# Decay-delta attention with a gated expert: chunks of 32 tokens, one batch per strip of partitions

## The chip, the cores and the metric

The kernel runs on one core of a Trainium2 chip. The metric is the device time of one launch in microseconds (us), median of several runs. TensorE (PE) multiplies, VectorE (DVE), ScalarE (ACT) and GpSimd (POOL) work on elements, and all transfers are issued from the queue of SyncE (SP).

## The reference

Two stages follow each other. The first is a recurrence over 768 tokens for each of 4 batches and 8 heads, with a state of 40 x 40 per head:

```python
y[:, :, t] = np.einsum('bhd,bhde->bhe', rt, state)
Sa = np.einsum('bhde,bhe->bhd', state, at)
state_decay = state * wt[:, :, None, :] - np.einsum('bhd,bhe->bhde', Sa, bt)
state = state_decay + np.einsum('bhd,bhe->bhde', vt, kt)
```

The second takes `y` as x of shape (4, 768, 320) and computes `h = relu(x @ w_in)` (1024 columns), a convolution of 3 taps along the tokens, `gate = sigmoid(conv)`, and `(h * gate) @ w_out` (320 columns). All in float32; the weights come as doubles.

## The kernel before

The recurrence is worked in chunks of C = 64 tokens. Inside a chunk the rule of the state is a unit triangular system for each head, so a chunk needs the scores of its tokens on each other, the inverse of a triangular matrix, a chain of products that carries the state on, and the outputs. A step takes one chunk of two batches; the four batches are two halves (`NP = 2`), worked one after the other, and there are 24 steps `m`, two to a window of 128 tokens.

- `scores` (L305 to L366): transposes of `k`, `b`, `a` on PE (`pk`, `pa`, `pz`), products `ps` of all 64 + 64 rows of `k` and `b` against `a` (L358), and `at`, masked on DVE (L363).
- `solve_in` and `solve` (L369 to L418): the diagonal blocks of 32 x 32 go from `at` to DRAM (`bd`, L373) and come back spread over partitions (`bb`, L381). 31 steps of elimination on POOL follow, each a product `st` (L402) and a sum `xx` (L408). The inverses go out (`xd`, L410) and come in as `tt` (L416).
- `chain` (L423 to L480): for one batch pair's half, the old state against `ah` (L436), the scores against `v` (L445), copy to `psb`, the inverse against that (L453), copy to `vu`. This is done for the first 32 tokens and again for the other 32, so each chunk has two such rounds. The state is then moved on with `pu` (L465, L473, L475).
- `outputs` (L484 to L566): `pr`, `pv`, `pt` are transposes, `pm` (L527) the scores of `r`, `py` (L541, L546) the outputs, `xf`, `xh`, `xl` the columns for the expert.
- `moe_in`, `moe_out` (L587 to L668): `ph` (L606) multiplies the window by both parts of `w_in`, `po` (L651) by both parts of `w_out`.

A product in float32 is two passes on PE, each with its own load of weights: 768 products at L453 are 1536 passes in the profile. Those of the expert, in a narrower float32 form, and the transposes take one pass.

Each part of a step is a generator that yields a few times. The dictionary `T` gives, for each kind of part, the step at which it is meant to stand; the parts are sorted by that and advanced in turn, which gives a first order. The framework's list scheduler then sets the order within each engine's queue (`schedule_with_timeline_sim=True`). Every engine works its queue in order, and so does SP's: a transfer that waits holds back those behind it. Buffers are rings (`bufs`), and a load waits until the readers of the buffer's last contents are done.

Of the kernel before, what the change touches and what calls it, by code (L numbers as in the profile page):

```python
# [17 lines left out]
C = 64  # L18
HB = 32
NZ = 4  # L20
NL = dict(w=1, a=1, r=2, kb=5, vu=3)
NWA = 5
NSUF, NPRE, NAT, NBB, NTT = 4, 6, 3, 2, 3
NAH, NKT, NAP, NVT, NRP, NSN, NMS, NRC = 7, 2, 2, 1, 1, 2, 2, 1
X = dict(k0=1, s0=0, xl=1, tg=0, rp=0, xx=1, cc=0)
NPS = dict(P=1, U=1, A=2, B=2, M=2)
T = dict(
    lwa=-3.686, lr=-0.08, dec=-3.09, lkb=-2.577, lv=-0.106, sc=-2.165, scb=0.413, scl=-0.145,
    so=-1.19, sol=0.564, chb=0.051, chl=0.412, ou=0.872, oub=0.433, oul=0.597, moe=4.134,
    moef=0.446, moel=0.444, mo0=0.197, moo=0.544, mwa=-1.3, mw0=-0.026, mw1=2.5, mop=0.324,  # L30
    decb=0.2,
)
GC = (0, 120, 200)
# [4 lines left out]
def tile_decay_delta_attention_then_conv_gate_moe(  # L38
# [19 lines left out]
    NB = 2  # L58
    NP = B // NB
    NW = S // (2 * C)  # L60
    NPAIR = NF // 2
    G = 3
    GR = 3 * D

# [3 lines left out]
    so = ctx.enter_context(tc.tile_pool(name="so", bufs=1))  # L68
    ch = ctx.enter_context(tc.tile_pool(name="ch", bufs=2))
    s1 = ctx.enter_context(tc.tile_pool(name="s1", bufs=2))  # L70
    mo = ctx.enter_context(tc.tile_pool(name="mo", bufs=2))
    gp = ctx.enter_context(tc.tile_pool(name="gp", bufs=4))
    dr = ctx.enter_context(tc.tile_pool(name="dr", bufs=2, space=DRAM))
    psP = ctx.enter_context(tc.tile_pool(name="psP", bufs=NPS["P"], space=PSUM))
    psU = ctx.enter_context(tc.tile_pool(name="psU", bufs=NPS["U"], space=PSUM))
    psA = ctx.enter_context(tc.tile_pool(name="psA", bufs=NPS["A"], space=PSUM))
    psB = ctx.enter_context(tc.tile_pool(name="psB", bufs=NPS["B"], space=PSUM))
    psM = ctx.enter_context(tc.tile_pool(name="psM", bufs=NPS["M"], space=PSUM))

# [15 lines left out]
    for q in range(2):  # L95
        nc.gpsimd.affine_select(
            out=tri[q * C : q * C + C, :], in_=tri[q * C : q * C + C, :],
            compare_op=ALU.is_ge, fill=0.0,
            base=-1, pattern=[[1, C]], channel_multiplier=-1,
        )  # L100
    xini = cp.tile([128, HB // NZ, HB], BF16, name="xini")
    nc.gpsimd.memset(xini, 1.0)
    for z in range(NZ):
        zs = slice(z * 128 // NZ, (z + 1) * 128 // NZ)
        nc.gpsimd.affine_select(
            out=xini[zs], in_=xini[zs], compare_op=ALU.is_equal, fill=0.0,
            base=-z, pattern=[[-NZ, HB // NZ], [1, HB]], channel_multiplier=0,
        )
    SL = C + 1
    NS = 2 * G  # L110
    dsuf = cp.tile([GR, NS * SL], BF16, name="dsuf")
    nc.vector.memset(dsuf, 0.0)
    nc.vector.memset(dsuf.rearrange("p (s c) -> p s c", c=SL)[:, :, C : C + 1], 1.0)
    dp0 = cp.tile([GR, NS * SL], F32, name="dp0")
    nc.vector.memset(dp0, 0.0)
    wxs = []
    for i in range(2):
        t = cp.tile([GR, NS * SL + 1], F32, name=f"wx{i}")
        nc.vector.memset(t, 0.0)
        wxs.append(t)  # L120

# [7 lines left out]
    def from_f64(raw, e, t, m):  # L129
        """Words of doubles (low, high) to float32, rounded to nearest; below its range to zero."""  # L130
# [29 lines left out]
    def load_moe_weights():  # L160
# [35 lines left out]
        # heads 5, 3, 4, 6, 7 of the low part move to where a row of x meets them (see moe_pack)  # L196
# [21 lines left out]
    def cols(bi, g):  # L218
        return slice(bi * H * D + GC[g], bi * H * D + GC[g] + GR)

    def src(x, p, lo, ln):
        xs = x[p * NB : (p + 1) * NB, :, lo : lo + ln, :]
        return xs.rearrange("b h t d -> t (b h) d")

    def flat(t):
        return t.rearrange("p h d -> p (h d)")

# [1 line left out]
    def hold(t):  # L229
        """The load of t comes after the first scores, which its bytes would delay."""  # L230
        nc.vector.tensor_copy(t[0:1, 0, 0:1], sts[0]["at"][0:1, 1, 0, 0:1])

    def load_wa(wd):
        p, n, t0 = wd["p"], wd["n"], wd["wi"] * 2 * C
        for x, nm in ((w, "w"), (a, "a")):
            t = ld.tile([128, NB * H, D], F32, tag=nm, bufs=NL[nm], name=f"{nm}n{n}")
            if n == 1 and nm == "w":
                hold(t)
            nc.sync.dma_start(t, src(x, p, t0, 2 * C))
            wd[nm] = flat(t)  # L240
        yield

    def load_r(wd):
        p, n, t0 = wd["p"], wd["n"], wd["wi"] * 2 * C
        t = ld.tile([128, NB * H, D], F32, tag="r", bufs=NL["r"], name=f"rn{n}")
        if n == 0:
            hold(t)
        nc.sync.dma_start(t, src(r, p, t0, 2 * C))
        wd["r"] = flat(t)
        yield  # L250

    def load_kb(st):
        wd, m = st["wd"], st["m"]
        t0 = wd["wi"] * 2 * C + st["c"] * C
        t = ld.tile([128, NB * H, D], F32, tag="kb", bufs=NL["kb"], name=f"kb{m}")
        if 1 < m < NL["kb"]:
            hold(t)
        nc.sync.dma_start(t[0:C], src(k, wd["p"], t0, C))
        nc.sync.dma_start(t[C:128], src(b, wd["p"], t0, C))
        st["kb"] = flat(t)  # L260
        yield

    def load_v(st):
        wd, m = st["wd"], st["m"]
        t0 = wd["wi"] * 2 * C + st["c"] * C
        t = ld.tile([128, NB * H, D], F32, tag="vu", bufs=NL["vu"], name=f"vu{m}")
        if 0 < m < NL["vu"]:
            hold(t)
        nc.sync.dma_start(t[0:C], src(v, wd["p"], t0, C))
        st["vu"] = flat(t)  # L270
        yield

# [1 line left out]
    def decays(wd, bi):  # L274
        n = wd["n"]
        pool, tag = (psM, "M") if n == 0 and bi == 1 else (psA, "A")
        pw = pool.tile([128, G, 128], F32, tag=tag, name=f"pw{n}{bi}")
        for g in range(G):
            nc.tensor.transpose(pw[:GR, g, :], wd["w"][:, cols(bi, g)], ident)
        wx = wxs[bi]  # L280
        nc.scalar.copy(
            wx[:, : NS * SL].rearrange("p (s c) -> p s c", c=SL)[:, :, 1:SL],
            pw[:GR].rearrange("p g (c t) -> p (g c) t", c=2),
        )
        yield
        suf = wn.tile([GR, NS * SL], F32, tag="suf", bufs=NSUF, name=f"suf{n}{bi}")
        nc.vector.tensor_tensor_scan(
            out=suf[:, ::-1], data0=wx[:, 1 : NS * SL + 1][:, ::-1],
            data1=dsuf[:, ::-1], initial=0.0, op0=ALU.mult, op1=ALU.add,
        )  # L290
        wd["suf"][bi] = suf.rearrange("p (g c t) -> p g c t", c=2, t=SL)
        nc.vector.reciprocal(
            dp0.rearrange("p (s c) -> p s c", c=SL)[:, :, 0:1],
            suf.rearrange("p (s c) -> p s c", c=SL)[:, :, 0:1],
        )
        pre = wn.tile([GR, NS * SL], F32, tag="pre", bufs=NPRE, name=f"pre{n}{bi}")
        nc.vector.tensor_tensor_scan(
            out=pre, data0=wx[:, : NS * SL], data1=dp0,
            initial=0.0, op0=ALU.mult, op1=ALU.add,
        )  # L300
        wd["pre"][bi] = pre.rearrange("p (g c t) -> p g c t", c=2, t=SL)
        yield

# [1 line left out]
    def scores(st, bi):  # L305
        wd, c, m, kb = st["wd"], st["c"], st["m"], st["kb"]
        sf = wd["suf"][bi]
        pool, tag = (psM, "M") if m == 0 and bi == 1 else (psA, "A")
        if bi == 0:
            st["at"] = wn.tile([128, NB, H, C], F32, tag="at", bufs=NAT, name=f"at{m}")  # L310
        wc = wn.tile([GR, G, 3], F32, tag=f"wc{bi}", bufs=NAT + 1, name=f"wc{m}{bi}")
        nc.vector.tensor_tensor(
            wc, sf[:, :, c, 0:1].to_broadcast([GR, G, 3]),
            hmask.unsqueeze(1).to_broadcast([GR, G, 3]), ALU.mult,
        )
        st["wc"][bi] = wc
        pk = pool.tile([128, G, 128], F32, tag=tag, name=f"pk{m}{bi}")
        for g in range(G):
            nc.tensor.transpose(pk[:GR, g, :], kb[:, cols(bi, g)], ident)
        if m == 0 and X["k0"]:  # L320
            kt = gp.tile([128, 512], F32R, tag="gl", name=f"kt{m}{bi}").bitcast(F32)
            kt = kt[:GR, : G * 128].rearrange("p (g t) -> p g t", g=G)
        else:
            kt = s1.tile([GR, G, 128], F32, tag="kt", bufs=NKT, name=f"kt{m}{bi}")
# [98 lines left out]
    def chain(st, nxt, bi):  # L423
# [35 lines left out]
        if last:  # L459
            yield  # L460
            return
# [378 lines left out]
```

## Time and profile before

Times of three runs: 833.13 us median, 832.01 to 842.79.

| the profiled execution | |
|---|---|
| span, first to last instruction | 831.5 us (1.6 below the median of the runs) |
| mean granted TensorE clock | 0.901 |
| PE busy, passes | 750.8 us (90%), 7645 |
| weight loads (PEld) busy | 667.7 us (80%) |
| DVE, ACT, POOL busy | 491.2, 404.5, 497.7 us |
| DMA packets, bytes | 237,619, 59.05 MB |

The page gives for each engine the time in which it was busy; a group's mean duration of an instruction on PE is its latency, and passes overlap, so that what a pass costs is read from groups that follow each other without a gap. SPq rows are the issuing of transfers on SP's queue.

### The profile page before, as it was taken

To read this page: it belongs to the slowest core of one execution; us is meant where nothing else is said; L and a number is where in the kernel's file an instruction comes from. 1 tells how busy PE (TensorE), PEld (TensorE's weight loads), DVE (VectorE), ACT (ScalarE), POOL (GpSimd) and SP (SyncE) were. 2 spreads that over 40 slices of the span, in tenths; PEclk is the share of its full clock that TensorE was granted. 3 is DMA by queue.
4 is the path that set the end of the run, shared out by engine and by line. 5 is a ranking of instruction groups with operands and counts; after the bars stand their busy time and mean duration, and the time that the engine had idled before them with its cause. 6 is when DMAs were issued, how large, how long until landed. Compare 5 with 4: busy or idle time off the path is not lost.

```text
span 831.5 us, 19927 instructions
## 1 busy us (share of the span) xinstructions
PE 750.8 (90%) x7645; PEld 667.7 (80%) x7645; DVE 491.2 (59%) x1236; ACT 404.5 (49%) x956; POOL 497.7 (60%) x1513
## 2 busy tenths in 40 slices
PE   5453969779988999999999999999799999999987
PEld 4343858669877889899898998898798998988986
DVE  6693858546545756666566476556366564663634
ACT  3121224336435646555556575465265465554644
POOL 1378885505888458787678478677655875781000
PEclk9555557897996999999999999999899999999989
DMA  8875453330441352532533543423334323211000
GB/s 140 136 150 93 102 91 59 59 74 17 88 85 30 67 103 59 99 68 48 106 68 60 101 81 74 89 56 77 64 65 86 73 43 74 53 21 30 10 17 25
DMA packets 237619, 59.05 MB, mean 71 GB/s; under 512 B 225788, under 2 KB 231828, under 8 KB 237524
## 3 DMA queue, kind: packets, MB, share of 16 engines
q1 hardware_dynamic: 237524, 57.78, 36.7%
q8 instruction: 60, 0.98, 0.5%
q14 instruction: 35, 0.29, 0.1%
HBM read 44.92 MB, written 10.22 MB: 66 GB/s over the span
## 4 chain that ended last, share of the span: by engine, by line
PE 69%; POOL 12%; DMA 11%; issue 3%; DVE 2%; ACT 1%; SPq 1%; ACTq 0%; POOLq 0%
PE ph L606 10%; PE po L651 9%; PE pp L453 7%; PE pp L445 7%; POOL xx L408 6%; POOL st L402 6%; PE ps L358 5%; PE py L546 5%; DMA xd<-xx 4%; PE pm L527 4%; PE py L541 3%; PE pu L465 3%; PE pp L436 3%; DMA tt<-xd 3%; PE pv L513 2%
## 5 line engine op out<-in xcount | busy, mean ns | idle before, releaser
L402 POOL TENSOR_TENSOR st<-xx,bb 128x60 f32<-128x60 f32 (+24 forms) x744 | 245.7, 331 | 159.7 <-DMA bb<-bd 95.5
L408 POOL TENSOR_TENSOR xx<-xx,st 128x60 f32<-128x60 f32 (+24 forms) x744 | 248.9, 336 | 54.5
L453 PE MATMUL pp<-psb,tt 32*32 32x40 f32 x1536 | 77.7, 205 | 29.3 <-DMA tt<-xd 28.8
L453 PEld LDWEIGHTS pp<-psb,tt 32*32 32x32 f32 x1536 | 65.7, 113 | 42.3 <-DMA tt<-xd 30.1
L457 ACT COPY vu<-pp 32x320 f32<-32x320 f32 x96 | 40.0, 417 | 95.1 <-PE pp L453 94.5
L450 ACT COPY psb<-pp 32x320 f32<-32x320 f32 x96 | 39.8, 415 | 88.8 <-PE pp L445 88.4
L502 DVE TENSOR_TENSOR rp<-pr,hmask 120x192 f32<-120x192 f32 x144 | 42.6, 350 | 65.0 <-PE pr L494 64.0
L445 PE MATMUL pp<-vu,at 96*32 96x40 f32 (+1 forms) x1536 | 78.3, 208 | 0.5 <-ACT vu L457 0.5
L445 PEld LDWEIGHTS pp<-vu,at 96*32 96x32 f32 (+1 forms) x1536 | 66.3, 116 | 12.5 <-issue 2.2
L358 PE MATMUL ps<-ap,kt 120*128 120x192 f32 (+1 forms) x288 | 66.6, 376 | 2.9 <-DVE kt L325 2.3
L344 ACT ACTIVATE ap<-ah,hmask 120x192 f32<-120x192 f32 x144 | 55.2, 445 | 23.2 <-DVE ah L337 20.3
L358 PEld LDWEIGHTS ps<-ap,kt 120*128 120x128 f32 x288 | 56.2, 227 | 6.8 <-DVE kt L325 2.7
L606 PE MATMUL ph<-xh,wih 120*128 120x256 f32 x288 | 56.6, 303 | 5.7 <-ACT xh L562 5.7
L546 PE MATMUL py<-kb,ms 128*64 128x40 f32 x768 | 57.4, 236 | 0.1
L546 PEld LDWEIGHTS py<-kb,ms 128*64 128x64 f32 x768 | 52.6, 145 | 3.5 <-issue 1.6
L527 PE MATMUL pm<-rp,vt 120*128 120x192 f32 (+1 forms) x288 | 53.3, 324 | 0.5 <-ACT sn L522 0.5
L629 DVE SCALAR_TENSOR_TENSOR cc<-hb,cw,cc 128x256 f32<-128x256 f32 x96 | 45.0, 496 | 11.4 <-ACT cc L625 11.4
L527 PEld LDWEIGHTS pm<-rp,vt 120*128 120x128 f32 x288 | 48.4, 199 | 1.1 <-ACT sn L522 0.8
L606 PEld LDWEIGHTS ph<-xh,wih 120*128 120x128 f32 x288 | 43.7, 198 | 6.8 <-ACT xh L562 6.0
L639 DVE TENSOR_TENSOR cc<-cc,hb 128x512 f32<-128x512 f32 x48 | 34.0, 713 | 21.8 <-ACT cc L638 21.4
L533 DVE TENSOR_TENSOR ms<-pm,tri 128x512 f32<-128x512 f32 x48 | 33.0, 688 | 22.4 <-PE pm L527 21.9
L633 DVE SCALAR_TENSOR_TENSOR cc<-hb,cw,cc 128x256 f32<-128x256 f32 x96 | 45.9, 495 | 0.0
(710 smaller groups left out, 1656.1 us busy)
## 6 DMA issues: line engine op xcount, KB each, us to landing
bb<-bd SPq DMA_DIRECT2D x24, 512.0 KB
wn<-in_w_dram SPq DMA_DIRECT2D x12, 320.0 KB
an<-in_a_dram SPq DMA_DIRECT2D x12, 320.0 KB
kb<-in_k_dram SPq DMA_DIRECT2D x24, 160.0 KB
kb<-in_b_dram SPq DMA_DIRECT2D x24, 160.0 KB
vu<-in_v_dram SPq DMA_DIRECT2D x24, 160.0 KB
rn<-in_r_dram SPq DMA_DIRECT2D x12, 320.0 KB
out_dram<-ob SPq DMA_DIRECT2D x20, 160.0 KB
```

Source lines behind the costliest of these rows:

```text
L344: nc.scalar.activation(out=ap[:, :, h, :], in_=ah, func=AF.Copy, scale=hmask[:, h : h + 1])
L358: nc.tensor.matmul(ps[:, h0 : h0 + hi - lo, :], kt[:, g, :], ap[:, g, lo:hi, :], start=(g == 0), stop=(g == G - 1), skip_group_check=True,)
L402: eng.tensor_tensor(t3, xx[:, 0:nj, i : i + 1].to_broadcast([128, nj, nt]), bb[:, i : i + 1, i + 1 :].to_broadcast([128, nj, nt]), ALU.mult,)
L408: eng.tensor_tensor(xx[:, 0:nj, i + 1 :], xx[:, 0:nj, i + 1 :], t3, ALU.add)
L445: nc.tensor.matmul(pp[rows, h, :], at[0:kr, bi, h, rows], vu[0:kr, o + h * D : o + (h + 1) * D], start=(first and h == 0), stop=True, skip ...
L453: nc.tensor.matmul(pp[urow, h, :], tt[rows, bi * H + h, :], psb[rows, h * D : (h + 1) * D], start=(h == 0), stop=True, skip_group_check=True,)
L527: nc.tensor.matmul(pm[:, h0 : h0 + hi - lo, :], vt[:, g, :], rp[:, g, lo:hi, :], start=(g == 0), stop=(g == G - 1), skip_group_check=True,)
L546: nc.tensor.matmul(py[0:C, h * D : (h + 1) * D], ms[:, h, :], kb[:, bi * H * D + h * D : bi * H * D + (h + 1) * D], start=(first and h == ...
L606: nc.tensor.matmul(ph[:, j], l[:, fs], x, start=(j == 0 and i == 0), stop=(i == len(passes) - 1), skip_group_check=True,)
L629: nc.vector.scalar_tensor_tensor(out=cc[:, j], in0=hb[:, j, :, 0:W], scalar=cw[:, 0, f : f + 1], in1=cc[:, j], op0=ALU.mult, op1=ALU.add,)
L633: nc.vector.scalar_tensor_tensor(out=cc[:, j], in0=hb[:, j, :, 2 : W + 2], scalar=cw[:, 2, f : f + 1], in1=cc[:, j], op0=ALU.mult, op1=ALU ...
L651: nc.tensor.matmul(po[:rows, :DM], l, rr[:, f, :], start=(m == 0), stop=(m == 3 * NF - 1),)
```

## The change

The chunk is now C = 32 tokens, and a step takes one chunk of all four batches. A tile of 128 partitions holds batch 0 in partitions 0 to 31, batch 1 in 32 to 63 and so on: one batch per strip of 32. There are again 24 steps; two consecutive ones are a pair that shares loads, scores buffer and inverses.

Products on PE that belong to one batch use only that batch's strip (rows, columns, or both, of PE's array) and are written with the batch as the innermost loop, so that consecutive products lie in different strips. This holds for the scores `ps` and `pm` (helper `against`, now L298), the chain `pp` (L439, L447), `pu` (L458), the state `pn` (L473) and the outputs `py` (L543, L552). A chunk has one round of the chain instead of two.

The triangular matrices are 32 x 32 and are inverted on POOL in 16 x 16 blocks: 15 steps (L377, L383) for a pair of chunks instead of 31 for each chunk. The new function `combine` joins the two blocks of each by two products, `pl` (L406) and `px` (L417), after a transpose on DVE (L398). The blocks travel in eight transfers each way (`bb` L363, `xd` L387); a full 32 x 32 matrix comes back as `tt` (L389). Every load of `w`, `a`, `k`, `b`, `v`, `r` is now eight transfers of 32 partitions (L242). The product of the state with the decay moves from DVE to POOL (L487), the masks of `rp` from DVE to ACT, and `xl` from DVE to POOL. PSUM is one ring of six banks for all of this (`psS`) and two for the expert. The expert's windows are 64 tokens of four batches instead of 128 of two.

The core of the diff:

```diff
-C = 64
-HB = 32
-NZ = 4
+C = 32
+HS = C // 2
...
+    lwa=-5.2, lkb=-4.8, lr=-1.2, lv=-1.6, dec=-3.4, sc=-3.2, scl=0.7, so=-1.8, sol=0.9, cm=-0.6,
...
+NPS = dict(S=6, M=2)
...
+    def fetch(x, pd, nm, held):
...
+        for bi in range(B):
+            for c in range(2):
+                nc.sync.dma_start(
+                    t[quad(bi), c],
+                    x[bi, :, t0 + c * C : t0 + c * C + C, :].rearrange("h t d -> t h d"),
+                )
...
+    def against(ps, x, lhs, mk, first):
+
         for g in range(G):
             lo, hi = GH[g]
...
+            for bi in range(B):
+                nc.tensor.matmul(
+                    ps[quad(bi), x, h0 : h0 + hi - lo, :], lhs[:, g, quad(bi)],
+                    mk[:, g, lo:hi, quad(bi)],
...
+    def solve_in(pd):
...
+        bb = buf(wn, [128, HS, HS], "bb", f"bb{j}")
+        for p0, q, bi in blocks():
+            qs = slice(q * HS, (q + 1) * HS)
+            nc.sync.dma_start(bb[p0 : p0 + 2 * H], bd[bi, qs, :, qs].rearrange("s h t -> h s t"))
...
+    def combine(pd):
+
+        j, at, tt = pd["j"], pd["at"], pd["tt"]
+        td = buf(wn, [128, 2, H, C], "td", f"td{j}")
+        nc.vector.transpose(
+            td.rearrange("p c h t -> p (c h t)"), tt.rearrange("p c h t -> p (c h t)")
+        )
+        pl = bank([128, 2, H, C], f"pl{j}")
+        for c in range(2):
+            for h in range(H):
+                for bi in range(B):
+                    rows = slice(C * bi, C * bi + HS)
+                    nc.tensor.matmul(
+                        pl[quad(bi), c, h, :], at[rows, c, 1, h, :], td[rows, c, h, :],
...
+        pu = bank([128, HD], f"pu{n}")
+        for h in range(H):
+            hc = slice(h * D, (h + 1) * D)
+            for bi in range(B):
                 nc.tensor.matmul(
-                    pp[urow, h, :], tt[rows, bi * H + h, :], psb[rows, h * D : (h + 1) * D],
+                    pu[quad(bi), hc], tt[quad(bi), c, h, :], psb[quad(bi), hc],
...
+                nc.vector.tensor_tensor(new, pn[bi][:GR], old[bi], ALU.add)
+                nc.gpsimd.tensor_tensor(n4, n4, w4, ALU.mult)
```

The order of PE's queue near the middle of the program, before: the state, the chain of the other half (`pp`) and the transposes and expert passes around them.

```order
L465 MATMUL pu_6213<-vu_5909,kb_4827 120x120 x3
L436 MATMUL pp_6406<-s_6201,ah_5363 64x120 x2
L436 MATMUL pp_6406<-s_6201,ah_5363 64x80
L445 MATMUL pp_6406<-vu_6379,at_5350 32x40 x8
L513 MATMUL pv_6640<-ident,vu_5909 120x128 x3
L556 MATMUL pq_6702<-ident,ysb_6618 120x64 x3
```

The same queue now, from the outputs of one step (`py`) through the chain's product with the inverse (`pu`) of the next to passes of the expert.

```order
L552 MATMUL py_7787<-k_3654,ms_7620 32x40 x32
L552 MATMUL py_7787<-b_3663,ms_7620 32x40 x32
L458 MATMUL pu_7890<-psb_7678,tt_7135 32x40 x32
L608 MATMUL ph_7990<-xh_5666,wih 128x256 x3
L608 MATMUL ph_7990<-xh_5666,wil 128x256
L608 MATMUL ph_7927<-xl_5667,wih 128x256 x2
```

Where eight products of one strip stood between changes of the array's layout, there are 32 that go round the four strips.

The order of SP's queue, before, from the inverses of one chunk on their way out (`xd`) to the blocks of a later chunk on their way in (`bb`).

```order
L410 DMA xd_4815<-xx_4152 4x256x32
L416 DMA tt_4817<-xd_4815 32x16x32 x2
L373 DMA bd_5097<-at_4884 32x16x32 x2
L248 DMA rn_5925<-in_r_dram 128x16x40
L381 DMA bb_5100<-bd_5097 128x1x1024
L269 DMA vu_5909<-in_v_dram 64x16x40
```

SP's queue now, for one pair, from its masked scores going out (`bd`) to its inverses coming back (`tt`).

```order
L356 DMA bd_7762<-at_6961 256x1x256
L242 DMA k_7143<-in_k_dram 32x8x40 x8
L242 DMA b_7152<-in_b_dram 32x8x40 x8
L363 DMA bb_7764<-bd_7762 16x16x16 x8
L586 DMA xl_6863<-xh_6862 40x256
L584 DMA xp_8763<-xh_6862 80x256
L585 DMA xp_8763<-xh_6862 40x256
L387 DMA xd_115<-xx_7773 16x16x16 x8
L668 DMA out_dram<-ob_8303 64x320 x2
L389 DMA tt_8331<-xd_115 128x512
```

Between `bd` and the transfers that wait for it there was one load, and there are now sixteen; `bb` and `xd` are eight transfers each instead of one.

The order of POOL's queue, before, in the middle of the elimination: only products and sums of that elimination.

```order
L408 TENSOR_TENSOR xx_4657<-xx_4657,st_0_4933 128x31
L402 TENSOR_TENSOR st_1_4936<-xx_4657,bb_4655 128x30
L408 TENSOR_TENSOR xx_4657<-xx_4657,st_1_4936 128x30
L402 TENSOR_TENSOR st_2_4939<-xx_4657,bb_4655 128x29
L408 TENSOR_TENSOR xx_4657<-xx_4657,st_2_4939 128x29
```

POOL's queue now, early in the elimination of a pair.

```order
L377 TENSOR_TENSOR st_2_6585<-xx_6577,bb_6568 128x39
L487 TENSOR_TENSOR s_6850<-s_6850,wc_5167 120x360
L383 TENSOR_TENSOR xx_6577<-xx_6577,st_2_6585 128x3x13
L487 TENSOR_TENSOR s_6853<-s_6853,wc_5167 120x360
L487 TENSOR_TENSOR s_6856<-s_6856,wc_5167 120x360
L377 TENSOR_TENSOR st_3_6588<-xx_6577,bb_6568 128x48
```

The state's products with the decay (`s`) now stand among the steps of the elimination.

More of the change, by code (lines that the diff above doesn't have):

```diff
@@ L263, in load_v, with cols @@
[L263 to L283, printed above, removed]
+    def cols(g):
+        return slice(GC[g], GC[g] + GR)
@@ L433, in chain @@
+    state = [None] * B
+    def chain(st, nxt):
+        n, c, pd = st["n"], st["c"], st["pd"]
+        at, tt, ah = pd["at"], pd["tt"], st["ah"]
+        kk, bk, vv = pd["k"][:, c], pd["b"][:, c], pd["v"][:, c]
+        first = n == 0
+        old = st["old"] = list(state)
+        pp = bank([128, HD], f"pp{n}")
         if not first:
@@ new lines, in outputs @@
+        for x, l in enumerate((kk, bk)):
+            for h in range(H):
+                hc = slice(h * D, (h + 1) * D)
+                for bi in range(B):
+                    nc.tensor.matmul(
+                        py[quad(bi), hc], ms[quad(bi), x, h, :], l[quad(bi), hc],
+                        start=(first and x == 0 and h == 0), stop=(x == 1),
+                        skip_group_check=True,
+                    )
+        ysb = buf(wn, [128, HD], "ysb", f"ysb{n}")
+        nc.scalar.copy(ysb, py)
@@ L719, in advance @@
         a[2] += 1
-    CUTS = (4, 8, 12, 16, 20, 24, 28)
-    early = [(("scores", 0, bi), 3) for bi in range(NB)]
+    CUTS = (4, 8, 12)
+    early = [(("scores", 1), 4)]
     for i in range(24):
```

737 lines of the change are left out of this document (340 added, 397 removed).

## The prediction

> **What bounds the kernel now.** I read the page first, then the windows, then the chain of waits from 300 us on, then the groups by form, then SP's and POOL's timelines. Rows of the page (engines' busy time, the chain by engine), and of the windows (PE, PEld, DVE, ACT, POOL busy, granted clock, DMA share, GB/s):
>
> ```profile
> PE 750.8 (90%) x7645; PEld 667.7 (80%) x7645; DVE 491.2 (59%) x1236; ACT 404.5 (49%) x956; POOL 497.7 (60%) x1513
> ...
> PE 69%; POOL 12%; DMA 11%; issue 3%; DVE 2%; ACT 1%; SPq 1%; ACTq 0%; POOLq 0%
> 0.00:100.00 100.00, 54.14 (x313) 45.00 (x313) 70.26 (x215) 27.56 (x67) 57.59 (x169) 0.60 0.68 127
> 100.00:200.00 100.00, 82.38 (x723) 72.59 (x721) 55.97 (x148) 38.21 (x96) 46.53 (x142) 0.72 0.37 65
> 400.00:500.00 100.00, 100.00 (x1105) 90.30 (x1101) 61.64 (x150) 58.60 (x137) 68.68 (x210) 1.00 0.43 82
> ```
>
> From 300 us on PE is busy all the time at the full clock; the other engines have a third of their time free. The first 200 us are filled less, at 0.60 and 0.72 of the clock. So the bulk goes by what PE's passes cost. I take that from the chain of waits, in groups that follow each other without a gap (start, us, line, passes):
>
> ```profile
> 304.34 0.69 PE pp L453 x16
> 308.88 0.69 PE pp L436 x6
> 314.99 0.88 PE pm L527 x6
> 321.47 1.07 PE ps L358 x6
> 358.02 1.44 PE ph L606 x12
> 378.37 0.91 PE py L546 x16
> 391.01 1.18 PE po L651 x8
> L453 PE MATMUL pp<-psb,tt 32*32 32x40 f32 x1536 | 77.7, 205 | 29.3 <-DMA tt<-xd 28.8 <-ACT psb L450 0.5
> L436 PE MATMUL pp<-s,ah 120*64 120x120 f32 x176 | 28.3, 285 | 0.6 <-ACT vu L457 0.5
> L527 PE MATMUL pm<-rp,vt 120*128 120x192 f32 x192 | 42.1, 344 | 0.5 <-ACT sn L522 0.5
> L358 PE MATMUL ps<-ap,kt 120*128 120x192 f32 x192 | 53.1, 408 | 2.9 <-DVE kt L325 2.3 <-ACT kb L352 0.5
> ```
>
> The last four rows are of the groups by form (weights, then operand, count). 16 passes of 40 columns are 640 columns and took 0.69 us; L436 is 4 x 120 + 2 x 80 = 640 columns, and took 0.69 us too. `pm` and `ps` are both 4 x 192 + 2 x 128 = 1024 columns; `pm`, which mostly follows a group in the same layout of the array, took 0.88 and `ps`, behind another layout, 1.07. So a float32 pass costs 0.88/1024 = 0.86 ns a column, and a change of layout about 0.14 us (0.69 - 640 x 0.86 ns; 0.19 for `ps`). `py` has 64 weight columns against 40 streamed: 0.91/16 = 57 ns a pass is 64 x 0.86, so the wider of the two counts. `ph` costs 0.12 us and `po` 0.148 us a pass.
>
> With these prices I count the whole program. Before, the float32 passes have 490,700 columns in this sense (counts and shapes of the groups by form; L453 above is 1536 x 40 of them): 422 us. 768 passes of `ph` and 600 of `po` and its kind: 181 us. 721 changes of layout: 101 us. The sum is 704 us, 29.3 a step; the chain gives 358.02 - 299.89 = 58.1 us for the two steps from one group of `ph` to its like:
>
> ```profile
> 299.89 1.44 PE ph L606 x12
> ```
>
> So 831.5 - 704 = 127 us of the span are start, end and stalls, most of them in the two first windows.
>
> **The change on PE.** The same count, for the program after: 790,900 columns in passes that use one strip, 680 us if they go one at a time; 116,200 columns of transposes, 100 us; the expert as before, 181 us; 290 changes of layout, 41 us. Together 1002 us, 41.8 a step. Nearly double the columns have two sources. A product of 120 rows by 128 columns becomes four by 32 columns, with the columns of the operand unchanged in sum for `ps` and `pm` but once for `k` and once for `b` (8192 a step for both against 4096); and `pn`, `py`, `pl`, `px` are done per batch (5520, 7573, 2048 and 2048 a step). What is removed is the other half of the rounds of the chain and 431 changes of layout, 60 us.
>
> So the forecast hangs on what passes in different strips cost when they follow each other, and the trace of before has no such neighbours: each of its groups stays in one place of the array. The bounds: above, no overlap at all (680 us, the 0.69 us row); below, all four strips at once (170 us). Between lies what the order forces. The two passes of one product stand next to each other and use the same strip, and the row of 16 passes in one place shows that these wait for each other. If passes start in the order of the queue, the second pass of a product holds back the next product, and overlaps only with that one's first pass. That halves the cost: 340 us. I take this, since it needs nothing but order. PE then has 340 + 100 + 181 + 41 = 662 us.
>
> The Trainium skill, page "TensorE: Matmul & The Clock Gate", section "Part 3: Packing small matmuls", has four row strips measured at 3.07 times one; by that the strips take 222 us and PE 543. No run here shows it yet.
>
> **The change on SP, POOL and the inverses.** The inverses of a pair lie on a loop of queues that PE's order closes: PE's `pl` waits for them, and the next pair's scores stand behind `pl` in PE's queue. Rows of SP's timeline (start, us, transfers), POOL's, and three groups:
>
> ```profile
> 508.10 0.97 SPq L373 DMA_DIRECT2D bd<-at  x2
> 510.57 0.97 SPq L381 DMA_DIRECT2D bb<-bd  x1
> 517.19 0.40 SPq L239 DMA_DIRECT2D an<-in_a_dram  x1
> 549.58 0.62 SPq L258 DMA_DIRECT2D kb<-in_k_dram  x1
> 551.00 0.59 SPq L410 DMA_DIRECT2D xd<-xx  x1
> 556.61 0.84 SPq L416 DMA_DIRECT2D tt<-xd  x2
> 394.84 0.38 POOL L408 TENSOR_TENSOR xx<-xx,st 128x66 f32<-128x66 f32 x1
> 402.68 0.20 POOL L402 TENSOR_TENSOR st<-xx,bb 128x8 f32<-128x8 f32 x1
> L363 DVE TENSOR_TENSOR at<-ps,tri 128x512 f32<-128x512 f32 x48 | 31.3, 685 | 17.7 <-PE pp L445 16.0 <-PE ps L358 1.5
> L408 POOL TENSOR_TENSOR xx<-xx,st 128x66 f32<-128x66 f32 x48 | 18.8, 393 | 3.8
> L408 POOL TENSOR_TENSOR xx<-xx,st 128x8 f32<-128x8 f32 x24 | 5.0, 209 | 0.1
> ```
>
> A transfer of 32 partitions takes 0.84/2 = 0.42 us to issue (`tt`), with its gap 0.43; others 0.40 (128 partitions) and 0.62 (64). `bd` has landed when `bb` is issued, 1.5 us after its issue ended; `xd` 5.0 us after (551.59 to 556.61). POOL's 20 rows from 394.84 to 402.68 make 19 steps of 0.41 us. For the product with the decay (360 elements) POOL has no row; the line through 8 and 66 elements gives 1.3 us as a mean, the shortest rows in the timeline about 0.8; I take 1.0.
>
> From the scores of a pair's second chunk to `pl`, after the change:
> - `at` on DVE 0.7; issue of `bd` 0.5; the sixteen loads of `k` and `b` queued between `bd` and `bb`, 16 x 0.43 = 6.9 (in their shadow `bd` lands);
> - eight `bb`, 3.4, and 1.5 to land: 4.9;
> - 30 instructions of the elimination, 30 x 0.41 = 12.4, and four state products that stand among them, 4.0;
> - eight `xd`, 3.4, landing 3.3 (between 1.5 and 5.0): 6.7; `tt` 0.4 + 1.5: 1.9; the transpose on DVE 0.7 (as `at`).
>
> The sum is 38.7 us, call it 39. Bounds: 27.5 without loads and state products in the way and with 1.5 for each landing, 48 with 0.62 an issue, 1.3 a product and 5.0 for each wide landing.
>
> What covers it is the PE work between those scores and `pl`. Counted over the rows of pair 7: 35,456 strip columns, 4,896 others, 20 passes of `ph`, 48 of `po`, 15 changes, so 15.8 us + 30.5 us divided by the overlap; with halves 31.1. From `pl` to the next such scores it is 10.9 us + 26.9 divided, 24.4. A pair's PE work is then 55.5 and the loop 39 + 24.4 = 63.4: PE stalls 8 us a pair, 12 x 8 = 96 us. At 27.5 the stall is nil, at 48 it is 17 us a pair, 205 us.
>
> **The rest.** The 127 us of start and end I keep. The first chain starts late because of the first inverses:
>
> ```profile
> 78.54 1.27 PE L453 MATMUL pp<-psb,tt 32*32 32x40 f32 x16 [7.23 <-DMA tt<-xd]
> ```
>
> Now 32 loads are needed before a pair's scores instead of five, and some 70 transfers stand ahead of the first `bd`: 70 x 0.43 = 30 us where `bd` went out at 17.5; the elimination is shorter by 31 - 15 steps for the first chunk, 32 x 0.41 = 13 us, and `bb` is half as large. About even, within 25 us. The other engines don't become the bound: POOL loses 1128 of 1488 elimination instructions and gains 88 products; ACT goes from 956 to about 730 instructions, DVE from 1236 to 1035, at the sizes of today or twice these. None comes near 662 us. SP issues 905 transfers instead of 339: at 0.43 to 0.62 that is 390 to 560 us of its queue, not the bound, but seldom idle.
>
> The sum: 662 + 127 + 96 = 885 us against 831.5 for the same sum before; the runs' median lies 1.6 us above that span, less than I can tell. With the loop's ends it is 789 to 994.
>
> **Rivals.**
> - *Strips don't overlap.* The change does not get what its order provides for. 1002 + 127 = 1129 us; the loop (39 + 37.8) hides behind 84 us of PE a pair. For it: nothing in the trace shows two passes in the array at once. Against it: loads of weights do run beside passes (PEld is busy 80% beside PE's 90%), so the array's parts are not locked together. 13%.
> - *Weights bound it.* Passes overlap but loads of weights go one at a time, at 0.86 ns a column (the 57 ns of `py` at 64). Then narrow products cost 2 x 32 x 0.86 = 55 ns instead of 34 (halved) or 69, `pn` stays at 114 us, only `ps`, `pm` and L439 are halved. Strips: 293 for passes of 32-column weights, 114 for `pn`, 110 for the wide ones, 517; PE 839, the loop just hidden (70 against 70 a pair): 966 us. 20%.
> - *Strips overlap three or four ways.* The queue runs ahead of a held pass. Strips take 227 or 170 us, PE 549 or 492, but the loop then decides: 39 + 19.8 against 45.7 stalls 13 us a pair (833 us in all), 39 + 17.6 against 41 stalls 15.6 (806). With the loop at 27.5 they give 695 and 669. This is the side of a gain, and it needs a short loop as much as the overlap. 32%.
>
> The Trainium skill's "TensorE: Matmul & The Clock Gate", section "Back-to-back issue gap", has a floor of about 25 ns a matmul up to 64 columns. For the 10,700 passes of 40 columns or fewer that is 267 us instead of 173 halved, which is a case between the forecast and the second rival: 662 + 94 + 127 + a stall of 46 = 929. The trace agrees only so far that no group goes below 36 ns a pass.
>
> **How the numbers follow.** Halves with a loop of about 39 has 35%, and gives 885. A measurement of this kernel tells 2%, 816 to 850 us, from no change. Faster needs three or four ways with a loop under 39 or so (three quarters of 32%) or halves with a loop near 29 (6%): 30%. No change takes 12%, from the same two. Slower is the rest, 58%. The range leaves out the first rival at the top and the shortest loops with full overlap at the bottom, some 20%: 745 to 1060.
>
> **What would show it.** In the profile after: the time of a group `pu` x64 in the chain (1.3 us halved, 2.3 alone, 0.7 four ways); 1.8 us for `pu` and 4.7 for `pn` would be the weights. The wait of PE's `pl`, or of POOL's first `st`, on a DMA would show the loop, 8 us a pair; with PE busy above 95% from 300 us on, the loop is hidden. The forecast is wrong if passes of one product in a strip don't hold back the next, or if other waits (six PSUM banks in one ring, `psb` and `u` single copies in the chain) stall PE beyond these.

## The result and the profile after

The changed kernel takes 933.31 us (median of 4 runs, 930.77 to 938.11), the kernel before 837.46 us beside it: a ratio of 1.115, 95% interval 1.107 to 1.123. It is slower. The profiled execution has a span of 930.2 us, with a mean granted TensorE clock of 0.803 (before: 0.901).

From the page of the changed kernel, its busy times and the chain by engine:

```profile
PE 631.3 (68%) x16941; PEld 563.6 (61%) x16941; DVE 430.5 (46%) x1035; ACT 338.4 (36%) x732; POOL 207.6 (22%) x505
PE 32%; SPq 17%; POOL 13%; DMA 12%; issue 10%; DVE 10%; ACT 5%; POOLq 0%; DVEq 0%; ACTq 0%
```

From its windows: PE, PEld, DVE, ACT, POOL busy, granted clock, DMA share, GB/s:

```profile
400.00:500.00 100.00, 76.83 (x2105) 69.29 (x2094) 43.43 (x95) 38.93 (x85) 21.20 (x47) 0.83 0.28 49
```

From PE's waits: what it waited for, us in total, times, longest:

```profile
PE pl L406 <- DVE td L398: 92.5, 10, 26.4
PE pp L439 <- POOL s L487: 37.3, 21, 5.6
```

PE was busy all the time between 400 and 500 us before; now it is busy 77% of it, and no other engine half. PE's share of the chain that ended last fell from 69% to 32%; transfers and SP's queue took its place. The longest wait is that of `pl` for `td`, the inverses.

A turn is the way of one pair round the loop; landing is the time from a transfer's issue until its data have arrived. One turn on SP, from its timeline (start, us, transfers):

```profile
402.86 5.83 SPq L668 DMA_DIRECT2D out_dram<-ob  x4
417.20 1.10 SPq L242 DMA_DIRECT2D r<-in_r_dram  x2
418.35 3.41 SPq L242 DMA_DIRECT2D v<-in_v_dram  x7
421.87 4.71 SPq L242 DMA_DIRECT2D w<-in_w_dram  x8
426.68 4.67 SPq L242 DMA_DIRECT2D a<-in_a_dram  x8
431.40 0.45 SPq L242 DMA_DIRECT2D v<-in_v_dram  x1
431.89 4.06 SPq L242 DMA_DIRECT2D r<-in_r_dram  x6
436.06 0.57 SPq L356 DMA_DIRECT2D bd<-at  x1
436.73 5.23 SPq L242 DMA_DIRECT2D k<-in_k_dram  x8
442.06 3.85 SPq L242 DMA_DIRECT2D b<-in_b_dram  x8
445.95 4.94 SPq L363 DMA_DIRECT2D bb<-bd  x8
...
465.78 2.30 SPq L387 DMA_DIRECT2D xd<-xx  x5
468.19 2.13 SPq L668 DMA_DIRECT2D out_dram<-ob  x2
470.37 1.59 SPq L387 DMA_DIRECT2D xd<-xx  x3
```

From SP's waits:

```profile
SPq L242 <- PE pvt L513: 91.3, 10, 14.5
```

Between 408.69 and 417.20 SP's queue stands at a load of `r` that waits for PE's transposes. It and the 31 loads behind it take until 435.95, past the end of `at` at 432.31, and only then is `bd` issued.

The same turn in the chain of waits (start, us, what):

```profile
424.03 0.72 PE pp L447 x64
...
428.48 1.02 PE ps L298 x48
...
458.89 1.22 PE pp L447 x64
...
473.41 2.73 DMA tt<-xd
476.17 0.72 DVE td L398
477.02 1.93 PE pl L406 x128
```

The second scores of the pair end at 429.50 and `pl` starts at 477.02, 47.5 us later. 64 passes in four strips (L447) take 0.72 us, at a granted clock of 1.00; the next such group, at 458.89, has a clock of 0.50 and takes 1.22 us. From events of this kind I took the loop apart for eight pairs (the fourth to the eleventh), in mean us; three kernels of the experiments stand beside it:

| step | changed | e4 | e13 | e14 |
|---|---|---|---|---|
| `ps` ends to `at` done | 1.8 | 1.8 | 2.3 | 1.9 |
| to `bd` issued (SP) | 6.4 | 5.6 | 5.1 | 5.2 |
| to first `bb` (loads, landing) | 8.9 | 8.8 | 13.4 | 3.4 |
| `bb`, and to the first `st` | 6.7 | 6.7 | 6.9 | 5.7 |
| elimination with what stands in it | 12.5 | 10.8 | 11.1 | 14.9 |
| `xd`, and its landing | 6.9 | 5.5 | 6.3 | 6.5 |
| `tt`, landing | 2.9 | 2.7 | 2.8 | 3.0 |
| `td` to `pl` | 0.9 | 0.9 | 0.9 | 3.6 |
| **loop to `pl`** | 47.0 | 42.7 | 48.7 | 44.1 |
| `pl` to the next pair's second `ps` | 23.7 | 24.5 | 23.7 | 24.0 |

A pair thus takes 47.0 + 23.7 = 70.7 us.

### The profile page after: what moved, and what is told of

Same layout as the page of the kernel before. It is cut to its first block, busy times and chain, and to the rows that moved or that the text cites. A ratio compares the mean times of both kernels' runs of the same rounds, so it can differ in the third digit from the quotient of the medians.

```text
span 930.2 us, 37971 instructions
## 1 busy us (share of the span) xinstructions
PE 631.3 (68%) x16941; PEld 563.6 (61%) x16941; DVE 430.5 (46%) x1035; ACT 338.4 (36%) x732; POOL 207.6 (22%) x505
## 3 DMA queue, kind: packets, MB, share of 16 engines
q1 hardware_dynamic: 224404, 45.76, 26.9%
## 4 chain that ended last, share of the span: by engine, by line
PE 32%; SPq 17%; POOL 13%; DMA 12%; issue 10%; DVE 10%; ACT 5%; POOLq 0%; DVEq 0%; ACTq 0%
SPq L242 7%; PE ph L608 7%; POOL xx L383 5%; POOL st L377 5%; SPq L363 5%; SPq L387 4%; PE pn L473 4%; DMA tt<-xd 3%; PE ps L298 3%; POOL s L487 3%; DMA xd<-xx 2%; PE po L647 2%; PE pl L406 2%; DMA bb<-bd 2%; PE px L417 2%
## 5 line engine op out<-in xcount | busy, mean ns | idle before, releaser
L377 POOL TENSOR_TENSOR st<-xx,bb 128x15 f32<-128x15 f32 (+4 forms) x180 | 53.9, 299 | 225.8 <-DMA bb<-bd 138.5
L406 PE MATMUL pl<-td,at 16*32 16x32 f32 x1536 | 23.2, 228 | 112.4 <-DVE td L398 92.5
L406 PEld LDWEIGHTS pl<-td,at 16*32 16x32 f32 x1536 | 21.2, 141 | 115.3 <-issue 115.3
L398 DVE STREAM_TRANSPOSE td<-tt 128x512 f32<-128x512 f32 x12 | 8.5, 711 | 161.4 <-DMA tt<-xd 161.4
L487 POOL TENSOR_TENSOR s<-s,wc 120x360 f32<-120x360 f32 x88 | 68.9, 806 | 59.6 <-DVE s L486 59.6
L439 PE MATMUL pp<-s,ah 120*32 120x120 f32 (+1 forms) x552 | 35.5, 309 | 38.3 <-POOL s L487 37.3
L506 ACT ACTIVATE rp<-pr,hmask 120x384 f32<-120x384 f32 x72 | 36.5, 577 | 63.9 <-PE pr L503 63.9
L383 POOL TENSOR_TENSOR xx<-xx,st 128x15 f32<-128x15 f32 (+4 forms) x180 | 54.6, 303 | 13.1
L486 DVE TENSOR_TENSOR s<-pn,s 120x360 f32<-120x360 f32 x88 | 40.9, 525 | 26.5 <-PE pn L473 26.5
L439 PEld LDWEIGHTS pp<-s,ah 120*32 120x32 f32 x552 | 21.6, 131 | 49.1 <-POOL s L487 48.3
L626 DVE SCALAR_TENSOR_TENSOR cc<-hb,cw,cc 128x256 f32<-128x256 f32 x96 | 45.1, 503 | 10.1 <-ACT cc L622 9.9
L564 DVE TENSOR_TENSOR xf<-pq,pre 120x384 f32<-120x384 f32 x24 | 13.4, 557 | 74.5 <-PE pq L562 74.5
L323 ACT ACTIVATE ap<-ah,hmask 120x384 f32<-120x384 f32 (+1 forms) x72 | 36.5, 569 | 28.8 <-DVE ah L316 28.1
L608 PE MATMUL ph<-xl,wih 120*128 120x256 f32 x192 | 44.4, 310 | 0.7 <-issue 0.6
L622 ACT ACTIVATE cc<-hb,cw 128x256 f32<-128x256 f32 x96 | 44.1, 503 | 1.8 <-DVE g110l L577 0.8
L525 ACT COPY sn<-pt 120x360 f32<-120x360 f32 x92 | 37.7, 471 | 18.6 <-PE pt L523 18.6
```

Of the source, the lines that this page charges most:

```text
L377: nc.gpsimd.tensor_tensor(t3, xx[:, 0:nj, i : i + 1].to_broadcast([128, nj, nt]), bb[:, i : i + 1, i + 1 :].to_broadcast([128, nj, nt]), A ...
L383: nc.gpsimd.tensor_tensor(xx[:, 0:nj, i + 1 :], xx[:, 0:nj, i + 1 :], t3, ALU.add)
L406: nc.tensor.matmul(pl[quad(bi), c, h, :], at[rows, c, 1, h, :], td[rows, c, h, :], start=(c == 0 and h == 0), stop=True, skip_group_check= ...
L439: nc.tensor.matmul(pp[quad(bi), GC[g] + lo : GC[g] + GR], ah[:, g, quad(bi)], old[bi][:, g, lo:], start=(g == 0), stop=False, skip_group_c ...
L486: nc.vector.tensor_tensor(new, pn[bi][:GR], old[bi], ALU.add)
L487: nc.gpsimd.tensor_tensor(n4, n4, w4, ALU.mult)
```

## Experiments

Theory L is the prediction's loop of queues; the rival W is that PE's own work is slow. All ratios are to the kernel before, measured beside.

**The strips, undone (e1).** The batch becomes the outermost loop of every strip product, as in `pu`:

```diff
-        for h in range(H):
-            hc = slice(h * D, (h + 1) * D)
-            for bi in range(B):
+        for bi in range(B):
+            for h in range(H):
+                hc = slice(h * D, (h + 1) * D)
```

> Theory L (loop): in the changed kernel the time is set by the loop from a pair's scores over the inverses to pl (47.5 us from the end of its second ps to pl in the profile) and on to the next such scores (23.9 us), 71.4 us a pair; the rotation makes four strips work at once, so PE has slack. Without the rotation (batch as the outermost loop of each product, the same products) the strips go one at a time at 0.86 ns a column: the part between scores and pl becomes 15.8 + 30.5 = 46.3 us and stays hidden, the part from pl to the next scores becomes 10.9 + 26.9 = 37.8 us, so a pair takes about 85 us: 933 + 12 x 14 = 1100 us. Rival W (PE's work): strips do not overlap much even with the rotation, and PE is slow by its own work; then the order of the batches changes nothing, 933 us within 2%, and a group pu of 64 passes keeps its duration of about 1.0 to 1.2 us.

1082.88 us in a single run, so without an interval. From PE's waits:

```profile
PE pl L406 <- DVE td L398: 52.2, 7, 26.5
```

And a group of its chain:

```profile
391.65 2.06 PE pp L447 x64
```

The same 64 passes take 2.06 us instead of 0.72, both at a granted clock of 1.00, so the rotation overlaps strips 2.9-fold. From the fourth to the eleventh `pl` a pair takes 83 us, where 85 was expected. W falls.

**The state's product back on DVE (e4).**

```diff
-                nc.gpsimd.tensor_tensor(n4, n4, w4, ALU.mult)
+                nc.vector.tensor_tensor(n4, n4, w4, ALU.mult)
```

> The product of the state with the decay goes back from POOL to DVE, nothing else. Theory L: four products of 0.8 us leave POOL's queue between the steps of the elimination, which takes 13.3 us where its 30 instructions alone take some 9: 3 to 4 us a pair off the loop, 933 - 12 x 3.5 = 891 us. Rival W: the chain keeps its length and the time stays within 2% of 933.

903.64 us, ratio 1.085 (1.076 to 1.093). The loop is 4.3 us shorter, but only 1.7 us of that lie in the elimination, where L looked for 3 to 4: in the changed kernel only three of the four products fall into it on the mean, 2.4 us. `xd` is 1.4 us shorter because the order of SP's queue changed: two output transfers stood among the `xd` in four of the eight pairs of the changed kernel and in one of e4. `bd` is issued 0.8 us sooner. With 0.8 us more behind `pl`, a pair is 3.5 us shorter; that this is L's figure is in part luck.

**Loads in the loop: more, fewer (e11, e13, e14).** e11 issues each load of `k` twice, the second time into a buffer of its own.

> The changed kernel with each load of k issued twice, the second time into a buffer that nobody reads: eight transfers of 32 partitions more for each pair, in SP's queue with the loads that stand between the masked scores and bb. Theory L: each issue takes 0.45 to 0.49 us of SP's queue and all of them lie on the loop: 3.6 to 3.9 us a pair, 933 + 12 x 3.8 = 979 us. Rival: SP's queue has room (905 issues of 0.45 us are 410 us in 930), 933 us within 2%.

953.87 us, 1.146 (1.138 to 1.153). This is neither L's 979 us nor the rival's 933 within 2%, and it doesn't test L: with no reader to wait for, all extra loads were issued by 210 us. The first `pl` came at 76 instead of 67 us and the third at 226 instead of 198; from the fourth to the eleventh a pair takes 69.7 us, where it takes 71.3 in the changed kernel. In e13 the extra loads wait for the masked scores:

```diff
+        nc.vector.tensor_copy(ex[:, :, 0, 0:1], at[:, :, 1, 0, 0:1])
+        for bi in range(B):
+            for c in range(2):
+                nc.sync.dma_start(ex[quad(bi), c], k[...])
         bb = buf(wn, [128, HS, HS], "bb", f"bb{j}")
```

> In e11_extra_loads the eight extra loads of a pair had nothing to wait for and were issued at the program's start, so they were not on the loop. Here eight extra loads a pair, into a buffer that nobody reads, depend on the pair's masked scores (one element a partition is copied from them on DVE first), so that they stand in SP's queue between bd and bb. Theory L: 8 x 0.49 = 3.9 us a pair on the loop: 933 + 12 x 3.9 = 980 us, 965 to 990. Rival: the loads in that place hide behind something else, 933 us within 2%.

947.96 us, 1.144 (1.133 to 1.155). In e14 a fourth buffer takes most loads out of that place:

```diff
-    w=1, a=1, r=2, k=3, b=3, v=2, suf=2, pre=6, al=2, wc=4, at=3, ah=4, ...
+    w=1, a=1, r=2, k=4, b=4, v=2, suf=2, pre=7, al=2, wc=5, at=3, ah=5, ...
```

> The changed kernel with only the buffers of e3_ahead (a fourth of k and b, one more of pre, ah and wc, one less of sn, two of wx): nothing stands earlier in the plan. With a fourth buffer the loads of k and b don't wait for the outputs of the pair three before, and in SP's queue most of them leave the place between bd and bb (3 of 16 stay there, some pairs have 8 ahead of bd). Theory L: some 10 issues of 0.49 us less on the loop: 933 - 12 x 5 = 873 us, 860 to 900. Rival: the buffers themselves change nothing, 933 us within 2%.

910.5 us, 1.100 (1.092 to 1.109). The directions are L's, the sizes of the time about a third: 15 of 47 us more, 23 of 60 less. By the time alone e13 lies within the rival's 2%, and the intervals of e14 and the changed kernel (1.107 to 1.123) just touch.

The case for L rests on the table: the way from `bd` to `bb` grew by 4.5 us in e13 and shrank by 5.5 in e14, where L had 3.9 and 4.9. The elimination then made up for part of it. In e13 fewer of the state's products fell into it (0.7 us of them instead of 2.4), and it took 11.1 us instead of 12.5. In e14 it took 14.9: the products 0.5 us more, `xl` in four of the eight pairs 0.5 on the mean, and its own 30 instructions 9.9 us instead of 8.3. All 39 of these instructions in e14's trace that took over 0.15 us more than the shortest of their form ran beside an instruction on DVE (in the changed kernel 17 of 17); that DVE is the cause was not tried. In e14 `pl` waits 2.7 us more for its turn as well.

**Loads on ACT's queue (e2, e7).**

```diff
-                nc.sync.dma_start(
+                nc.scalar.dma_start(
                     t[quad(bi), c],
```

> All loads of w, a, k, b, v, r are issued from ACT's queue, the transfers of the inverses stay on SP's. Theory L: the 4.4 us between the masked scores and bd and some 7 of the 9.9 us between bd and bb go, so the loop is about 11 us a pair shorter: 933 - 12 x 11 = 800 us. ACT issues 48 loads a pair, some 20 us of its queue, and a copy of the chain can come late by a few us behind them, so up to 850. Rival W (PE's work, not the loop): 933 us within 2%.

996.53 us, 1.200 (1.189 to 1.210): slower yet, and outside L's 800 to 850. On the mean of the same eight pairs `at` to the first `bb` took 3.0 us instead of 15.3, as L wanted, but `pl` came 9.9 us behind `td` instead of 0.9, and from `pl` to the next second `ps` it took 32.7 us instead of 23.7. ACT's timeline in e2:

```profile
446.96 3.92 ACTq L242 DMA_DIRECT2D w<-in_w_dram  x8
450.98 3.92 ACTq L242 DMA_DIRECT2D a<-in_a_dram  x8
454.93 0.47 ACT L261 COPY wx<-pw 120x372 f32<-120x372 f32 x1 [8.05 <-DMA a<-in_a_dram]
```

PE's waits in e2:

```profile
PE pm L298 <- ACT wx L262: 51.4, 8, 8.2
PE pq L562 <- ACT ysb L558: 42.0, 9, 7.4
```

ACT's copies `wx` stood behind sixteen issues that had waited for their buffers. In e7 only `k` and `b` move.

> Only the loads of k and b go to ACT's queue; those of w, a, v, r stay on SP's. Theory L: between bd and bb nothing is left, the 9.9 us become about 3 (bd's landing), 6.5 us a pair: 933 - 12 x 6.5 = 855 us. Rival, after e2_loads_act: the sixteen issues wait in ACT's queue for their buffers and hold up copies that PE waits for; then 930 or more.

937.61 us, 1.131 (1.120 to 1.143): not L's 855, and the rival's 930 or more. PE's waits in e7:

```profile
PE pq L562 <- ACT ysb L558: 68.5, 9, 11.5
```

`bb` followed `bd` by 3.4 us on the mean, as wanted, but now `ysb` stands behind the issues in ACT's queue, and PE behind `ysb`: `pl` came 9.1 us behind `td` instead of 0.9. The wait changed its queue.

**The loop spread over two pairs (e3, e5, e6).** e3 moves loads, decays, scores and elimination one step ahead in the plan (`sc=-4.2`, `so=-2.8` and so on), with e14's buffers.

> Loads, decays, scores and elimination stand one step earlier in the plan, with a fourth buffer of k and b and one more of pre, ah and wc (one less of sn and two of wx to make room): the scores of a pair's second chunk now stand before pl of the pair before in PE's queue, so that the loop spans two pairs. Theory L with strips four ways: the loop no longer binds (71 us for two pairs), PE's own work of about 492 us and start and end of 127 give 620; with other waits 620 to 760. Theory L with halves: 662 + 127 = 790. Rival W: 933 us within 2%. If the buffers of k and b bind in place of the loop: 850 to 930.

944.09 us, 1.136 (1.125 to 1.147): no gain at all. L's 620 to 790 failed, and the time alone is what W said (933 within 2%); PE's waits name another cause:

```profile
PE put L513 <- DVE s L486: 99.3, 16, 14.7
```

And from its chain:

```profile
436.82 2.67 DMA tt<-xd
440.22 0.50 DVE s L486
440.77 0.89 PE put L513 x3
```

PE's order had been opened, but in DVE's queue `td` still stood ahead of the state's sum: it waited for `tt`, and the sum and all of PE behind it waited with it. e5 places `td` a step later by a copy that needs a newer state:

```diff
+        if state[0] is not None:
+            nc.vector.tensor_copy(td[0:1, 0, 0, 0:1], state[0][0:1, 0, 0:1])
         nc.vector.transpose(
```

> The kernel of e3_ahead, where the loop had closed again through DVE's queue: the transpose td stood there waiting for tt, ahead of the state's sum s, for which PE's put and so all behind it waited (99 us). Here a copy of one element from the state two chunks back stands ahead of td and takes the same buffer, so that td comes one step later in DVE's queue. Theory L: the loop then spans two pairs in all queues, a pair takes PE's own 45 to 55 us, 670 to 770 us in all. Rival: yet another queue holds a transfer of the inverses in front of the work that feeds the next one, and the pair keeps its 71 us: 900 to 950 us.

882.71 us, 1.065 (1.055 to 1.076); 64 us a pair, between L's 670 to 770 us and the rival's 900 to 950. The longest wait of PE is now that of `pp` for the state on POOL, 60.4 us in 22 waits. e6 adds the edit of e4.

> As e5_ahead_hold, and the state's product with the decay on DVE as in e4_state_dve. Theory L: with the loop out of the way the length of the elimination no longer counts, so the time is that of e5_ahead_hold within 2%. Rival: if the loop still binds there, this takes another 3 us a pair, 35 us, off, as e4_state_dve took 30.

863.02 us, 1.041 (1.031 to 1.051); 63 us a pair. That is 2.2% below e5, just outside L's 2%, and 20 of the rival's 35 us; whether the shorter elimination or the wait of `pp` for POOL gave them was not separated. From SP's waits in e6:

```profile
SPq L387 <- POOL xx L383: 166.2, 12, 16.5
```

And from SP's timeline:

```profile
462.32 4.58 SPq L363 DMA_DIRECT2D bb<-bd  x8
467.00 1.12 SPq L670 DMA_DIRECT2D out_dram<-ob  x2
483.82 5.54 SPq L387 DMA_DIRECT2D xd<-xx  x8
491.14 0.35 SPq L389 DMA_DIRECT2D tt<-xd  x1
491.54 0.92 SPq L242 DMA_DIRECT2D r<-in_r_dram  x2
```

SP's queue now goes round by itself: `xd` waits 16 us for POOL at its head, and the loads behind it start only at 491.54.

**The inverses' transfers on POOL's queue (e9, e10, e12).** `bb`, `xd` and `tt` are issued by POOL, which waits for these blocks in any case:

```diff
-            nc.sync.dma_start(bb[p0 : p0 + 2 * H], ...)
+            nc.gpsimd.dma_start(bb[p0 : p0 + 2 * H], ...)
```

> The changed kernel with the transfers bb, xd and tt issued from POOL's queue instead of SP's; order of the work as it was. Theory Q (in-order queues): a transfer of the inverses that waits on SP holds up loads, and loads hold up the transfers; on POOL's queue, which waits for these blocks anyway, the 16 loads leave the way from bd to bb (9.9 us become about 2.5), some 7 us a pair: 933 - 12 x 7 = 850 us, if POOL issues a transfer in about the 0.45 us that SP takes. At 1 us an issue the 17 of a pair give back 9 us: 930 us or more. Rival: the state's product with the decay stands in POOL's queue behind waits for bb and tt, so that the chain waits instead: over 950 us.

894.15 us, 1.083 (1.076 to 1.090): 39 of the 83 us. From POOL's timeline:

```profile
435.43 4.47 POOL L363 DMA_DIRECT2D bb<-bd  x8 [18.76 <-DMA bd<-at]
```

POOL issues a transfer in 4.47/8 = 0.56 us, and `bd` still waits on SP behind other loads (`at` was done at 425.79, `bd` issued at 432.68).

> As e6_ahead_hold_dve, with bb, xd and tt on POOL's queue. In the profile of e6_ahead_hold_dve, a pair takes 63 us, and SP's queue goes round without a gap: bd, bb, then xd, which waits up to 17 us for POOL with the 32 to 48 loads of later pairs behind it (166 us of waits of xd in all). Theory Q: that queue is what is left of the loop; without xd and tt in it SP has 35 us of issues a pair, and a pair takes PE's 50 us (80% of 63): 863 - 12 x 12 = 720 us, 700 to 780. Rival (PE's chain of products, state and copies with its own waits): 840 to 870 us.

798.08 us, 0.966 (0.959 to 0.974): faster than both kernels. A pair takes 56 us, and PE is busy 85% of this window at a clock of 0.91:

```profile
400.00:500.00 100.00, 84.98 (x2659) 76.85 (x2649) 58.66 (x126) 46.03 (x101) 45.90 (x100) 0.91 0.34 63
```

It lies between Q's 700 to 780 and the rival's 840 to 870: PE still waits in many small places, the state's sums on DVE between the expert's among them.

> As e10_ahead_pool, but bb, xd and tt of the first pair alone stay on SP's queue. In the profile of e10_ahead_pool the first tt stood in POOL's queue behind the second pair's bb and the first pl came at 85.9 us, in e6_ahead_hold_dve at 67.7 us. If the start is on the path: 798 - 15 = 783 us, 778 to 790. If the second pair then waits as long: 798 us within 1%.

802.17 us, 0.962 (0.956 to 0.969): as e10, the rival's 1%. The first `pl` came 19 us earlier, the third again at 194 us (e10: 190). The first pair's inverses don't set the time.

**The clock (e8).** 64 unread products ahead of `pl` keep PE busy where it waited:

```diff
+            for _ in range(64):
+                nc.tensor.matmul(pl[...][:, 0:256], wih[:, 0, 0:128], wih[:, 0, 0:256], ...)
```

> From the third pair on, PE does 64 products of 120 x 128 by 256 columns that nobody reads (7.7 us at full clock) ahead of pl, where it waits about 9 us for td. Theory C: the granted clock falls to half because PE waits there, and the passes from pl to the next scores run at half speed for some 5 us of work; with PE kept busy they don't, and the loop's second part goes from 23.9 to 18 or 19 us: 933 - 10 x 5 = 880 us. Rival: the clock has other reasons, and the added work costs what it takes beyond the wait: 933 to 970 us.

946.89 us, 1.143 (1.129 to 1.156), in the rival's range. The windows around `pl` of the changed kernel:

```profile
405.00:410.00 5.00, 2.51 (x131) 2.31 (x131) 1.48 (x3) 0.95 (x2) 0.00 (x0) 0.65 0.21 55
410.00:415.00 5.00, 4.47 (x195) 4.01 (x194) 1.68 (x3) 0.58 (x2) 1.00 (x1) 0.67 0.03 6
```

The same windows of e8:

```profile
405.00:410.00 5.00, 5.00 (x134) 4.74 (x135) 1.48 (x3) 1.29 (x3) 0.40 (x1) 1.00 0.27 89
410.00:415.00 5.00, 5.00 (x44) 5.00 (x44) 0.00 (x0) 0.00 (x0) 0.00 (x0) 1.00 0.15 38
```

And from PE's waits in e8:

```profile
PE pp L445 <- POOL s L493: 50.2, 26, 8.0
```

The clock did rise there, from 0.65 to 1.00. On the mean of the eight pairs `pl` took 1.3 us from its first to its last pass instead of 3.0. But from the end of `pl` to the next second `ps` it took 20.6 us instead of 20.7 (in the turn shown 22.2 instead of 20.1), with more waits of the chain for the state on POOL (50.2 us in all, 37.3 in the changed kernel), and the added products let `pl` start 3.8 us after `td` instead of 0.9. So C's 18 to 19 us were not reached (21.9 instead of 23.7), and a pair was no shorter. What the low clock costs by itself was not shown.

## Why the prediction was right and where it was wrong

**Direction, bound and place were right.** It forecast 885 us in a range of 745 to 1060; the kernel took 933. PE's work did not set the time; the loop of the inverses did, `pl` waiting for `td` in PE's queue, as the text had it. But the forecast rise was about 50 us and the measured one 96: a term of the loop's sum failed, and with it the size. The overlap was wrong too, and cost little.

**The sum of the loop (39 us) was mis-sized; it measured 47.0.** The step that failed is "issue of `bd` 0.5" right behind `at`: it took SP's queue to be free then, and put the wait for it at nothing. In place of that, `bd` was issued 6.4 us after `at` on the mean. In seven of the eight pairs `a`, `v` and `r` loads stood right in front of it (rows above), in the other `k` and `b` too. In each of the eight, SP's queue had first stood 8.5 to 14.2 us at a load of `r` that waited for PE's transposes. That the loads would have been out of the way without this wait is argued from the rows; more buffers of `r` and `v` were not tried.

Of the other terms, the wait of `at` on DVE is 1.1 us longer, the loads 1.5, `bb` 1.8, `tt` 1.0, `xd` and `td` 0.2 each. The elimination is 3.9 us shorter than summed (12.5 for 16.4): the products with the decay take 2.4 us in it for 4.0, three of 0.8 us on the mean, and its 30 instructions with their gaps 10.1 for 12.4. The upper bound of 48 is near by chance, since it came from longer issues, landings and products and has no wait of `bd`.

**The overlap (halves) was wrong.** The text argued that the second pass of a product holds back the next product. It does not: 64 passes take 0.72 us, where it gave 1.3 halved and 0.7 four ways. The four-way rival had the price. The Trainium skill, page "TensorE: Matmul & The Clock Gate", section "Part 3: Packing small matmuls", has 3.07 for four row strips and 512 columns; e1 over the changed kernel gives 2.06/0.72 = 2.9 for 40 columns, so the trace agrees with the page and not with the text's argument. That page's floor of about 25 ns a matmul (section "Back-to-back issue gap") was counted per pass in the text; a pass took 0.72/64 = 11 ns here, a product of two passes 22, so it does not hold for these strips. The time hardly shows it, since the loop binds: the second part of a turn, forecast 24.4 us with halves, measured 23.7. That they agree is luck: at an overlap of 2.9 the text's own terms give 10.9 + 26.9/2.9 = 20.2, and the rest is lower clock (0.65 in the window shown) and waits for POOL.

**Start and end were 20 us too long.** The text gave 885 - 12 x 63.4 = 124 us beside the pairs. The profile has the first `pl` at 67.1 and the last at 824.4, 68.8 us a pair on the mean of eleven, and 930.2 - 12 x 68.8 = 105. The forecast had the pairs 65 us too short and the rest 20 us too long, which hid a part of the miss.

**Rivals.** No overlap would have been 1129 us; without the rotation the kernel takes 1083, 4% less. Weights one at a time would have shown 1.8 us for a group like `pu`; at a clock of 1.00 L447, of the same shape, takes 0.72. The side of a gain "needs a short loop as much as the overlap": e10 has both and is the only case, with e12, below the kernel before.

## What to carry to other kernels

When a change makes the bounding engine's work cheaper, add up the longest loop that runs through several in-order queues, and for each transfer in it ask what stands in front of it in its queue, not only what it waits for. Opening such a loop in one queue moves it to the next (PE's, then DVE's, then SP's here), so each queue on the way has to be opened before the loop stops binding; until then what helps is to shorten it (e4, e9, e14). A transfer that waits is best tried in the queue of the engine that waits for it anyway: that paid in e9 and e10, while loads moved to an engine with other work (e2, e7) did not.

## What the runs showed of the hardware

- Products in four strips overlap 2.9-fold if consecutive ones lie in different strips (11 ns a pass of 40 columns), even though both passes of each lie in one strip; the same products batch by batch take 32 ns a pass.
- The granted clock fell to 0.65 after PE had waited for `td` and was 1.00 there once PE had other work; a pair was no shorter by it. The same 64 passes took 0.72 us at 1.00 and 1.22 us at 0.50.
- An issue took 0.45 us on SP's queue and 0.56 us on POOL's.
- In e10 one copy on POOL took 9.75 us, beside 0.4 us in the changed kernel. DVE was busy in all of that stretch, with 36 instructions back to back; that this held up the copy was not tried. The copy in POOL's timeline of e10, and the stretch in e10's windows:

```profile
75.66 9.75 POOL L365 CAST xx<-xini 128x256 f32<-128x256 bf16 x1
75.66:85.41 9.75, 0.00 (x0) 0.00 (x0) 9.75 (x36) 1.62 (x4) 9.75 (x1) 0.50 0.80 158
```
